# A fused attention and feed-forward kernel: the first pixel chunk loaded uncast through SyncE and cast in SBUF

## The chip, the cores and the metric

The kernel runs on one core of one Trainium2 chip. The core has five engines with a queue of instructions each: TensorE (PE in the profile; PEld is its weight loads), VectorE (DVE), ScalarE (ACT), GpSimd (POOL) and SyncE (SP). SP issues transfers through a hardware queue (q1 in the profile), POOL through a software queue (q0) whose descriptors POOL itself writes; POOL's transfers may change the data type on the way, for instance from float32 to bfloat16. Both queues move their bytes with the same 16 DMA engines. The metric is device time of one execution in microseconds (us), and lower is better.

## The reference

```python
B, C, Hh, Ww = (4, 128, 384, 32)          # q: (B, Hh*Ww, C), kv: (B, Hh, Ww, C), w_sr: (C, C)
kv_pool = kv.reshape(B, H // 4, 4, W // 4, 4, C).mean(axis=(2, 4))
k = v = kv_pool.reshape(B, -1, C) @ w_sr
s = scale * (q @ k.transpose(0, 2, 1))    # scale = 1 / sqrt(C)
a = softmax(s)
x = (a @ v).reshape(B * N, C)             # 49152 tokens
h = x @ w_in                              # w_in: (128, 2048)
out = (h * sigmoid(1.702 * h)) @ w_out    # w_out: (2048, 128)
```

Each image of pixels (`kv`) is averaged in blocks of 4 by 4, which gives 768 keys of 128 channels per image; keys and values are the same matrix. All inputs and the output are float32. The kernel works in bfloat16, with float32 sums.

## The kernel before

**The work.** Queries come in 96 groups of 512 tokens (four groups make a tile of 2048), keys in 6 chunks of 128 per image. For each pair of a group and a key chunk PE makes a 128x512 block of scores (L340), ACT takes the exponential of one to three blocks at once (L342), and PE multiplies the result with the values (L353). DVE divides by the sums and writes the tokens into the large SBUF array `x` (L376 and L379). The second half does the same with the feed-forward layer: PE fills (L586), ACT applies the activation (L588), PE multiplies with the second matrix (L596). The work runs in two rounds (`R = 2`): attention for half of the groups, then their feed-forward, then both once more. Between them the tokens of a round go to DRAM in blocks of 24 x 128 tokens and come back transposed (`put_away`, L493, and `bring_back`, L499, both on SP's queue).

**The order.** The order of every engine's instructions is fixed when the program is built: the list `seq` holds the fills in ACT's order, `first` holds the jobs that are done ahead of each of the first fills, and a small model of times (`now`, `free`, `COST`) places the rest. Waits are put in by the framework where data depend on each other. Each transfer that POOL or SP issues also takes one of eight semaphores in turn, and waits for the transfer that used the same one before.

**The start, which the change touches.** Image 0 comes in six chunks of pixels, `load_chunk(b, jc)` (L126 to L131). A chunk is 128 rows of 2048 values: POOL's transfer reads 1 MB of float32 and writes 512 KB of bfloat16 into a slot of `x`. `XS` is 12, a slot is `SG` = 2048 columns, and chunk `jc` lies in slot 11 - `jc`. Slots 3 to 5 hold the first queries, and slots 0 to 2 hold nothing until attention writes its results there. SP loads the key layer's matrix `w_sr` (L242). POOL issues, in this order (L243 to L256): chunk 0, the queries' first group, their second, chunk 1, two more pieces of queries of two groups each, chunks 2 to 5, more queries, and two casts of queries to DRAM.

While these are under way, DVE builds the identity `ident` from a row of numbers (`row`) and a column (`col`), 32 x 32 at a time (L269 to L273), the mask `sum4` that adds four neighbouring rows (L275 to L277), and the scaled matrix `w_sr_sb` (L279). PE runs 13 warm-up matmuls (`warm(13)`, L291). Then come the jobs of `first`: `pool_chunk(0, 0)` makes 16 matmuls (L139), four (`w`) for each of four blocks of pixel columns (`wp`); DVE copies the sums (L142); `transpose_q(0)` turns the first queries (L233), which ACT copies (L237); `key_chunk` makes the first keys (L148, L149); and so on to the first scores (L340) and exponentials (L342). Chunk 1 is pooled (`pool_chunk(0, 1)`) ahead of the third fill.

**Put away.** `put_away(n, m)` moves block `m` of round `n` in one transfer (768 KB), or in the first round for `m` over `FIRST` = 3 in two of half the size.

Of the kernel before, what the change touches and what calls it, by code (L numbers as in the profile page):

```python
# [7 lines left out]
F32 = mybir.dt.float32  # L8
# [4 lines left out]
AX = mybir.AxisListType  # L13
ADD = mybir.AluOpType.add
MUL = mybir.AluOpType.mult
GE = mybir.AluOpType.is_ge
LE = mybir.AluOpType.is_le
SUB = mybir.AluOpType.subtract
MAX = mybir.AluOpType.max
# [5 lines left out]
def kernel(  # L25
    ctx, tc, q, kv, w_sr, moe_w_in, moe_w_out, out,
):
    nc = tc.nc
    B, N, C = q.shape
    _, H, W, _ = kv.shape  # L30
    r = 4
# [7 lines left out]
    SG = 4 * G  # L39
# [13 lines left out]
    kv_r = kv.rearrange("b (ch p) (a w) c -> b a ch p (w c)", p=128, a=2)  # L53
# [6 lines left out]
    XS = NS // R  # L60
# [24 lines left out]
    def acc(key=None):  # L85

        nonlocal last_acc
        last_acc = next_acc()
        turns.append(last_acc)
        turns.remove(last_acc)  # L90
        if key:
            closes[last_acc] = key
        return banks[:, last_acc, :]
# [15 lines left out]
    x = xpool.tile([128, XS * SG], BF, name="x")  # L109

    def x_tile(s):
        return x[:, s % XS * SG:(s % XS + 1) * SG]
# [5 lines left out]
    kv_tiles, kv_sums, pooled, pTs, kTs, vs = {}, {}, {}, {}, {}, {}  # L118
# [7 lines left out]
    def load_chunk(b, jc):  # L126

        a, ch = divmod(jc, HC)
        t = x_tile(XS - 1 - jc)
        nc.gpsimd.dma_start(out=t, in_=kv_r[b, a, ch])  # L130
        kv_tiles[b, jc] = t.rearrange("p (wp w1 c) -> p w1 wp c", w1=r, c=C)  # L131

    def pool_chunk(b, jc):

        ps = acc()
        t = kv_tiles.pop((b, jc))
        for wp in range(4):
            for w in range(r):
                nc.tensor.matmul(ps[:, 32 * wp:32 * wp + 32], t[:, w, wp, :], sum4,  # L139
                                 start=(w == 0), stop=(w == r - 1))  # L140
        pTs[b, jc] = kvtmp.tile([128, 128], BF, name="pTc", bufs=2)
        nc.vector.tensor_copy(pTs[b, jc], ps[:, 0:128])  # L142
# [78 lines left out]
    def load_q(s, lo, hi):  # L221
        nc.gpsimd.dma_start(
            out=qs[s].rearrange("p (g e) -> p g e", g=4)[:, lo:hi, :],
            in_=q_flat[s * SG + lo * G:s * SG + hi * G, :].rearrange("(g p i) c -> p g (i c)", p=128, i=4))

    def transpose_q(g):
# [11 lines left out]
        else:  # L238
            nc.vector.tensor_copy(dst, src)

    w_sr_f = cpool.tile([128, C], F32)
    nc.sync.dma_start(out=w_sr_f, in_=w_sr)  # L242
    load_chunk(0, 0)  # L243
    load_q(0, 0, 1)
    load_q(0, 1, 2)
    load_chunk(0, 1)
# [14 lines left out]
    col = cpool.tile([128, 32], F32)  # L261
# [3 lines left out]
    row = cpool.tile([128, 32], F32)  # L265
    nc.vector.transpose(row, col)
    ident = cpool.tile([128, 128], BF)
    nc.vector.memset(ident, 0.0)
    for m in range(0, 128, 32):  # L269
        p = slice(m, m + 32)  # L270
        nc.vector.tensor_tensor(ident[p, p], row[p], col[p], EQ)
        if m > 0:
            nc.vector.tensor_scalar_add(row[p], row[p], float(m))  # L273
    sum4 = cpool.tile([128, 32], BF)
    nc.vector.scalar_tensor_tensor(row, col, -float(r), row, MUL, ADD)  # L275
    nc.vector.tensor_scalar(col, row, 0.0, None, GE)
    nc.vector.scalar_tensor_tensor(sum4, row, r - 1.0, col, LE, MUL)  # L277
    w_sr_sb = cpool.tile([128, C], BF)
    nc.vector.tensor_scalar_mul(w_sr_sb, w_sr_f, 1.0 / (r * r))  # L279

# [63 lines left out]
    def drain_attn(t, a):  # L344
# [18 lines left out]
        if k == TS - 1 and a == 1:  # L363
            close(("av", u), max(now, dve - 1.0) + EVACUATE)
            on_dve(6.5 if split else 4.3)
            ps = av_of.pop(u)[:, 0:TS * (C + 1)]
            if split:
                part = parts[:, u, 0:TS * (C + 1)]
                nc.vector.tensor_tensor(part, ps, part, ADD)
                ps = part  # L370
                if u == SPLIT - 1:
                    kept = 0
                    order.clear()
            ps = ps.rearrange("p (k c) -> p k c", k=TS)
            rec = npool.tile([128, TS], F32, name="rec")
            nc.vector.reciprocal(rec, ps[:, :, C])  # L376
            n, o = divmod(u * TS, RT)
            to = x[:, o * T:(o + TS) * T].rearrange("p (k c) -> p k c", k=TS)
            nc.vector.tensor_tensor(to, ps[:, :, 0:C], rec.unsqueeze(2).broadcast_to([128, TS, C]), MUL)  # L379
            if n and (o + TS) % PART == 0:  # L380
                m = o // PART
                put_away(n, m)
                if m:
                    bring_back(n, m - 1)
                if m == RT // PART - 1:
                    bring_back(n, m)
# [100 lines left out]
    PART, FIRST = 24, 3  # L487

    def put_away(n, m):
        size = PART // 2 if n == 0 and m > FIRST else PART  # L490
        for o in range(m * PART, m * PART + PART, size):
            lo = n * XS * SG + o * T
            nc.sync.dma_start(out=x_bf[lo:lo + size * T, :].rearrange("(k p) c -> p k c", p=T),  # L493
                              in_=x[:, o * T:(o + size) * T].rearrange("p (k c) -> p k c", k=size))
# [22 lines left out]
    def background(i):  # L517

        first_round = i < GB * 2
        s = TURN.get(i, NS) if first_round else i // 4 + 3 if i % 4 == 0 else NS  # L520
        if s < NS:
            load_qT(s)
        if i in CAST:
            gate()
            for s in CAST[i]:
                cast_q(s)
        if i in (10, 12):
            gate()
            for jc in range(i % 10 * 3 // 2, i % 10 * 3 // 2 + 3):
                load_chunk(1, jc)  # L530
        if 0 <= i - 16 < JC:
            extras.append((key_and_value, 1, i - 16))
        if 0 <= i - 15 < JC:
            extras.append((pool_chunk, 1, i - 15))
        if i in (28, 33, 38):
            put_away(0, (i - 28) // 5)
        if i in (31, 36, 41):
            bring_back(0, (i - 31) // 5)
        if i == 27:
            gate()  # L540
            nc.gpsimd.dma_start(out=w_in_sb, in_=moe_w_in)
        if i == 28:
            gate()
            nc.gpsimd.dma_start(out=w_out_sb, in_=moe_w_out.rearrange("(o p) c -> p o c", p=128))

    def background_moe(g):

        n, g = divmod(g, 4 * XS)
        m, odd = divmod(g - 9, 2)
        m += FIRST  # L550
        if n == 0 and FIRST <= m < RT // PART:
            (bring_back if odd else put_away)(n, m)
        g += n * 4 * XS
        nonlocal low
        if g == 12:
            low = EARLY * JC
            order[:] = [f for f in order if f >= low // K]
        if g in CAST_MOE:
            gate()
            cast_q(CAST_MOE[g])  # L560
        if g in (41, 42):
            load_qT(g - 28)
        if g == 43:
            background(early[0])
        for b, lo in ((2, 2), (3, 24)):
            if lo <= g < lo + 8:
                gate()
                add_kv(b, g - lo)
            if g in (lo + 10, lo + 12):
                use_kv(b, (g - lo - 10) // 2)  # L570
# [76 lines left out]
    for n in range(R):  # L647
        part = [c for c in chunks if c[0] // (NG // R) == n]
        while part:
            m = sizes.pop(0) if sizes else K  # L650
# [12 lines left out]
        while flat:  # L663
            m = K if len(flat) > sum(rest) else rest.pop(0)
# [36 lines left out]
    def prepare(p):  # L701
# [12 lines left out]

    first = {
        0: [(pool_chunk, 0, 0), (transpose_q, 0), (warm, 1), (key_chunk, 0, 0), (transpose_q, 1)],
        1: [(value_chunk, 0, 0), (warm, 1)],
        2: [(pool_chunk, 0, 1), (warm, 2), (key_and_value, 0, 1), (warm, 1), (transpose_q, 2)],
        3: [(transpose_q, 3)],
        4: [(transpose_q, 4)],  # L720
# [66 lines left out]
    for n in range(len(seq)):  # L787
        fill(n + 2)
        jobs(n + 3)
        while True:  # L790
# [33 lines left out]
            kind, i, c = source[0]  # L824
# [58 lines left out]
```

The softmax here doesn't subtract the row's maximum and nothing guards it: scores larger than these inputs give would overflow.

## Time and profile before

| what | us |
|---|---|
| median of 4 runs (951.1 to 951.33) | 951.22 |
| the profiled execution's own time | 951.1 |
| its span, first to last instruction | 949.3 |
| PE busy / ACT busy | 936.0 / 934.0 |
| DVE busy / POOL busy | 537.0 / 67.1 |
| chunk 0 from POOL's issue at 1.27 to its landing | 5.4 |
| other chunks, issue to landing, median | 10.3 |
| put away, 768 KB / 384 KB, issue to landing, median | 5.9 / 4.6 |

The profile covers one execution of the program. Its page gives each engine's busy time, DMA queues, the chain of work that ended last, and the costliest groups of instructions. Of any stretch one can ask for the list of instructions in order of time (start, length, engine, line, operation, output and inputs, count; in brackets how long the engine had been idle and what released it), for the chain of waits, for each group's mean duration by shape, for busy times by window, and for what the DMA engines moved in 40 equal slices. "L139" is line 139 of the kernel. A matmul's end is modelled, so neighbouring matmuls overlap in the list. DMA sizes and rates count the bytes as written.

### The profile page before, as it was taken

The page shows a single profiled execution, that of the slowest core. Times are in us where ns is not written, and L with a number is a line of the kernel's source. Part 1 is how long each engine was busy: PE and PEld are TensorE (multiplying, and loading weights), DVE is VectorE, ACT ScalarE, POOL GpSimd, SP SyncE. Part 2 cuts the span into 40 slices and gives each one's busy share as a digit, 9 for nine tenths or more (in the row PEclk, how much of TensorE's full clock was granted, in tenths as well). Part 3 has the DMA queues.
Part 4 walks back from the last instruction along what each step waited for, and adds up shares of the span by engine and source line. Part 5 has one row for each costly group of instructions (what it writes and reads, how often), then busy time and mean ns, then how long its engine had stood idle before and what let it go on. Part 6 is the DMA issues. An engine that isn't in the chain of part 4 may idle for free.

```text
span 949.3 us, 15311 instructions
## 1 busy us (share of the span) xinstructions
PE 936.0 (99%) x6201; PEld 503.0 (53%) x6314; DVE 537.0 (57%) x1037; ACT 934.0 (98%) x708; POOL 67.1 (7%) x115
## 2 busy tenths in 40 slices
PE   8999999999999999999999999999999999999998
PEld 4677776444444444444446777754444444444444
DVE  5643553102477777778655775465666665566631
ACT  5999999999999999999999999999999999999998
POOL 4101001330000242000000000000000000000000
PEclk9999999999999999999999999999999999999999
DMA  9999922999766899765335583562222222222222
GB/s 182 207 176 193 212 59 41 157 125 180 153 133 102 126 146 126 123 103 77 66 55 112 131 162 76 135 122 34 44 34 45 34 46 34 45 33 45 34 45 45
DMA packets 372871, 94.93 MB, mean 100 GB/s; under 512 B 346736, under 2 KB 370416, under 8 KB 372464
## 3 DMA queue, kind: packets, MB, share of 16 engines
q1 hardware_dynamic: 343872, 61.31, 36.8%
q0 software_dynamic: 28656, 32.51, 22.5%
q8 instruction: 49, 0.80, 0.4%
q14 instruction: 22, 0.18, 0.1%
q10 hardware_dynamic: 272, 0.13, 0.0%
HBM read 52.49 MB, written 48.76 MB: 107 GB/s over the span
## 4 chain that ended last, share of the span: by engine, by line
ACT 88%; PE 9%; DMA 2%; issue 1%; DVE 0%; POOL 0%; POOLq 0%
ACT ag L588 71%; ACT ag L342 17%; PE banks L340 4%; PE banks L353 3%; DMA qT<-q_bf 1%; DMA x<-in_kv_dram 1%; PE banks L139 0%; PE banks L586 0%; PE banks L624 0%; ACT L588 0%; PE banks L233 0%; PE banks L596 0%; ACT L342 0%; DVE kT L163 0%; PE banks L161 0%
## 5 line engine op out<-in xcount | busy, mean ns | idle before, releaser
L588 ACT ACTIVATE ag<-banks 128x1536 bf16<-128x1536 f32 (+1 forms) x510 | 682.2, 1508 | 0.0
L586 PE MATMUL banks<-x,w_in_sb 128*128 128x512 bf16 x1485 | 407.4, 379 | 2.0 <-ACT ag L588 0.3
L596 PE MATMUL banks<-ag,w_out_sb 128*128 128x512 bf16 x1476 | 403.2, 379 | 1.9
L342 ACT ACTIVATE ag<-banks 128x1536 bf16<-128x1536 f32 (+2 forms) x192 | 245.8, 1442 | 4.2 <-PE banks L233 2.6
L596 PEld LDWEIGHTS <-w_out_sb 128*128 128x128 bf16 x1520 | 148.5, 98 | 178.0 <-issue 0.9
L586 PEld LDWEIGHTS <-w_in_sb 128*128 128x128 bf16 x1522 | 147.3, 98 | 170.4 <-issue 1.1
L607 DVE STREAM_TRANSPOSE o_sb<-banks 128x512 f32<-128x512 f32 x95 | 67.9, 715 | 210.7 <-PE banks L596 195.7
L353 PEld LDWEIGHTS <-ag 128*128 128x128 bf16 x2272 | 146.1, 98 | 46.3 <-issue 0.6
L353 PE MATMUL banks<-v,ag 128*128 128x129 bf16 x2272 | 163.7, 220 | 0.2
L340 PE MATMUL banks<-qT,kT 128*128 128x512 bf16 x499 | 145.0, 379 | 3.5 <-DVE kT L163 1.0
L432 DVE SCALAR_TENSOR_TENSOR ea<-ea,eb 128x512 f32<-128x512 f32 x128 | 87.9, 686 | 3.2
L376 DVE RECIPROCAL rec<-banks 128x3 f32<-128x3 f32 x124 | 22.3, 180 | 95.9 <-PE banks L353 95.9
L379 DVE TENSOR_TENSOR x<-banks,rec 128x384 bf16<-128x384 f32 x124 | 69.2, 558 | 4.3
L340 PEld LDWEIGHTS <-kT 128*128 128x128 bf16 x544 | 46.3, 98 | 26.5 <-DVE kT L163 1.7
L463 DVE RECIPROCAL eb<-ea 128x256 f32<-128x256 f32 x28 | 47.6, 1726 | 0.5
L173 POOL DMA_DIRECT2D kvs<-in_kv_dram x32 | 40.5, 1315 | 19.8 <-DMA kvs<-in_kv_dram 16.3
L421 DVE TENSOR_SCALAR ea<-banks 128x512 f32<-128x512 f32 x32 | 22.1, 692 | 33.1 <-PE banks L405 32.8
L456 DVE SCALAR_TENSOR_TENSOR ea<-ea,eb 128x512 f32<-128x512 f32 x56 | 38.3, 684 | 1.6
L511 POOL MEMSET gate_tile<- 1x1 f32 x37 | 3.9, 105 | 324.6 <-DVE gate_tile L510 324.6
L427 DVE SCALAR_TENSOR_TENSOR eb<-eb,ea 128x512 f32<-128x512 f32 x32 | 22.1, 690 | 0.9
L443 DVE TENSOR_SCALAR qT<-banks 128x512 f32<-128x512 f32 x14 | 9.7, 692 | 17.2 <-PE banks L399 16.9
L434 DVE SCALAR_TENSOR_TENSOR ag<-ea,ee 128x512 bf16<-128x512 f32 x24 | 16.5, 688 | 0.7
(84 smaller groups left out, 267.8 us busy)
## 6 DMA issues: line engine op xcount, KB each, us to landing
out_dram<-o_sb SPq DMA_DIRECT2D x380, 64.0 KB, 2.0
kvs<-in_kv_dram POOLq DMA_DIRECT2D x32, 384.0 KB, 6.4
q_bf<-in_q_dram POOLq DMA_DIRECT2D x21, 512.0 KB, 6.7
x_bf<-x SPq DMA_DIRECT2D x12, 768.0 KB, 5.9
x<-in_kv_dram POOLq DMA_DIRECT2D x12, 512.0 KB, 10.3
x_bf<-x SPq DMA_DIRECT2D x8, 384.0 KB, 4.6
x<-in_q_dram POOLq DMA_DIRECT2D x5, 256.0 KB, 15.5
w_in_sb<-in_moe_w_in_dram POOLq DMA_DIRECT2D x1, 512.0 KB, 10.2
```

The source lines that it names most:

```text
L173: nc.gpsimd.dma_start(out=kv_sums[b][:, i2], in_=kv_p[b, i, w, :, i2], **({"accum_op": ADD} if n else {}))
L340: nc.tensor.matmul(ps[:, k, :], kTs[i // GB][:, jc * 128:(jc + 1) * 128], rhs, start=True, stop=True)
L342: nc.scalar.activation(place([("a",) + c for c in chunks]), ps, AF.Exp, scale=scale)
L353: nc.tensor.matmul(av_of[u][:, k * (C + 1):(k + 1) * (C + 1)], weights(("a", i, jc))[:, o:o + T], vs[i // GB][:, jc, 0:C + 1], start=(jc = ...
L379: nc.vector.tensor_tensor(to, ps[:, :, 0:C], rec.unsqueeze(2).broadcast_to([128, TS, C]), MUL)
L432: nc.vector.scalar_tensor_tensor(a, a, COEFFS[k], b, ADD, MUL)
L456: nc.vector.scalar_tensor_tensor(a, a, COEFFS[k], b, ADD, MUL)
L463: nc.vector.reciprocal(b[:, m:m + 256], a[:, m:m + 256])
L586: nc.tensor.matmul(ps[:, k, :], w_in_sb[:, fc * 128:(fc + 1) * 128], x[:, g % (4 * XS) * G:(g % (4 * XS) + 1) * G], start=True, stop=True)
L588: nc.scalar.activation(place([("m",) + c for c in chunks]), ps, AF.Gelu_apprx_sigmoid)
L596: nc.tensor.matmul(o_of[g], w_out_sb[:, fc, :], weights(("m", g, fc)), start=(fc == 0), stop=(fc == FCH - 1))
L607: nc.vector.transpose(o_sb, o_of.pop(g))
```

## The change

Chunk 0 no longer comes through POOL's queue. SP's queue brings it uncast, 1 MB of float32, ahead of `w_sr`, into slots 0 and 1 of `x`, seen as float32. Once it has landed, five copies turn it into bfloat16 and put it where it was before: DVE casts columns 0 to 511, 512 to 1023 and 1792 to 2047, ACT casts 1024 to 1535 and 1536 to 1791. The blocks of pixel columns (`wp`) of this one chunk are pooled in the order 0, 2, 1, 3. The mask `sum4` is taken from `ident` with one maximum over four neighbouring columns, in place of six operations. In the first round, the put-away of block 4 goes in one transfer and only blocks over 4 go in two.

```diff
-        for wp in range(4):
+        for wp in (0, 2, 1, 3) if (b, jc) == (0, 0) else range(4):
...
+    first_f = x[:, 0:2 * SG].bitcast(F32)
+    nc.sync.dma_start(out=first_f, in_=kv_r[0, 0, 0])
     w_sr_f = cpool.tile([128, C], F32)
     nc.sync.dma_start(out=w_sr_f, in_=w_sr)
-    load_chunk(0, 0)
     load_q(0, 0, 1)
...
         nc.vector.tensor_tensor(ident[p, p], row[p], col[p], EQ)
-        if m > 0:
-            nc.vector.tensor_scalar_add(row[p], row[p], float(m))
     sum4 = cpool.tile([128, 32], BF)
-    nc.vector.scalar_tensor_tensor(row, col, -float(r), row, MUL, ADD)
-    nc.vector.tensor_scalar(col, row, 0.0, None, GE)
-    nc.vector.scalar_tensor_tensor(sum4, row, r - 1.0, col, LE, MUL)
+    nc.vector.tensor_reduce(sum4, ident.rearrange("p (j k) -> p j k", k=r), AX.X, MAX)
+
+    def cast_first():
+
+        t = x_tile(XS - 1)
+        for lo, hi, copy in ((0, 512, nc.vector.tensor_copy), (1024, 1536, nc.scalar.copy), (512, 1024, nc.vector.tensor_copy),
+                             (1536, 1792, nc.scalar.copy), (1792, 2048, nc.vector.tensor_copy)):
+            copy(t[:, lo:hi], first_f[:, lo:hi])
+        kv_tiles[0, 0] = t.rearrange("p (wp w1 c) -> p w1 wp c", w1=r, c=C)
+
+    cast_first()
     w_sr_sb = cpool.tile([128, C], BF)
     nc.vector.tensor_scalar_mul(w_sr_sb, w_sr_f, 1.0 / (r * r))
...
-        size = PART // 2 if n == 0 and m > FIRST else PART
+        size = PART // 2 if n == 0 and m > FIRST + 1 else PART
```

The order of PE's instructions is otherwise what it was, and so is that of ACT, DVE and POOL. On SP's queue one transfer is added at the front and one is gone at block 4.

## The prediction

> **What bounds the kernel now.** I read the page's busy shares first, then the list of ACT's instructions over the first 60 us, then the chain of waits over the first 13 us, and then DMA, PE, POOL and DVE in that stretch.
>
> ```profile
> PE 936.0 (99%) x6201; PEld 503.0 (53%) x6314; DVE 537.0 (57%) x1037; ACT 934.0 (98%) x708; POOL 67.1 (7%) x115
> ```
>
> ```profile
> 0.76 1.28 ACT L237 ACT_TABLE_LOAD   x1 [0.76 <-PEq L867]
> 7.77 0.58 ACT L237 COPY qT<-banks 128x512 bf16<-128x512 bf16 x1 [5.73 <-PE banks L233]
> 9.03 1.29 ACT L342 ACTIVATE ag<-banks 128x512 bf16<-128x512 f32 x2 [0.67 <-PE banks L340]
> 12.92 48.04 ACT L342 ACTIVATE ag<-banks 128x1024 bf16<-128x1024 f32 x44 [2.60 <-PE banks L233]
> ```
>
> The first four fields are start, length, engine and line; the bracket is the idle time before and its releaser. From 12.92 us on ACT runs without a gap that counts: all its waits in the span sum to 11.6 us (5.7, 2.6, 1.3, 1.2 and 0.8), of which 9.8 lie ahead of 12.92. The end is therefore 12.92 plus a sum of ACT work that the change leaves alone. What moves the third exponential (12.92) moves the end, one for one, as long as PE can keep up behind it.
>
> What puts it at 12.92? In the chain of waits (start, length, what) and in PE's list:
>
> ```profile
> 1.27 0.69 POOL x L130
> 1.96 1.03 POOL x L222 x2
> 2.99 7.44 DMA x<-in_kv_dram
> 10.43 0.05 issue
> 10.48 0.57 PE banks L139 x16
> ```
>
> ```profile
> 0.97 5.73 PE L284 MATMUL banks<-ones 128*32 128x512 bf16 x13 [0.97 <-DVE col L262]
> 6.68 0.58 PE L139 MATMUL banks<-sum,x 128*128 128x32 bf16 x16
> 9.30 0.39 PE L340 MATMUL banks<-qT,kT 128*128 128x512 bf16 x1
> 10.48 0.57 PE L139 MATMUL banks<-sum,x 128*128 128x32 bf16 x16 [0.79 <-DMA x<-in_kv_dram]
> ```
>
> It is the landing of the second pixel chunk at 10.43: PE had finished its last score matmul at 9.30 + 0.39 = 9.69 and stood 0.79 us before pooling that chunk. The first chunk is pooled at 6.68, where the 13 warm-up matmuls end. Their weight loads stand 0.43 us apart (the last three before the gap at 4.79, 5.21 and 5.64) and ends are modelled, so pooling could begin two steps after 5.64, at about 6.50, not before.
>
> The DMA view from 1 to 8 us, in 40 slices of 0.175 us:
>
> ```profile
> GB/s 0 0 0 0 67 228 79 0 0 70 164 70 70 23 23 117 164 211 140 281 234 211 187 211 164 211 234 170 146 170 199 205 193 205 211 263 240 222 234 257
> w_sr_f<-in_w_sr_dram SPq DMA_DIRECT2D x1, 64.0 KB, 1.8
> ```
>
> SP's key matrix moves from the fifth slice (1.7 to 1.9 us); POOL's queue starts in the tenth (2.6 to 2.75), crawls until 4.0 (88 GB/s over 2.6 to 4.0), then runs full. From 8 to 16 us the mean is 209 GB/s, and the bytes counted are the written ones (512 KB for a chunk): a cast chunk costs 524,288 / 209,000 = 2.51 us, a 128 KB query piece 0.63.
>
> **What the change moves, with prices.**
>
> *The transfer.* Chunk 0 leaves POOL's queue and becomes the first on SP's (0.76 issue, first bytes 1.8). POOL drops one issue of 0.69; its first query piece takes that place at 1.27, so its bytes still start near 2.65. Uncast it writes 1 MB. No row shows so large an uncast read, so bounds: if the reading side limits, it costs what the same 8 KB rows cost with the cast, 2.51 us; if the writing side, 1,048,576 / 209,000 = 5.02. Between lies the key matrix on the same queue: 3.4% of 7 us for 65,536 bytes is 0.238 us, 275 GB/s, or 3.81 us for 1 MB, but in rows of 512 B. I take 2.51, since rows, packets per engine and source are those of the cast chunk.
>
> From 1.8 to 2.7 it runs alone (0.9 of 2.51); 1.61 remain. If it keeps the engines it ends at 4.3; if it shares them half and half with POOL's queue, at 2.7 + 3.22 = 5.9. Completion adds 0.6 (before: 0.12 MB by 4.0 and the rest at 200 GB/s ends at 6.0, pooled at 6.68). Landing 4.9 to 6.5; I take the middle, 5.7. At 3.81 us with sharing: 2.7 + 5.8 + 0.6 = 9.1; at 5.02: 11.5.
>
> *The second chunk.* The same bytes' worth of work stands ahead of it, but work starts at 1.8 plus the matrix's 0.24 instead of 2.65, which brings 0.6 us; the crawl of POOL's queue (1.4 us at 88 instead of 209, so 0.8 us lost) can now lie under chunk 0, which would make 1.4. It lands at 10.43 less 0.6 to 1.4: 9.0 to 9.8.
>
> *The casts.* DVE's nearest rows are one-source operations in SBUF, 128x512: L429 0.421, L423 0.439 (from PSUM, L421: 0.692, the other end); a quarter of that size, L279, 0.219. So 0.42 + 0.42 + 0.29 for 256 columns = 1.13 us. ACT: 0.60 (its 512-column exponential, 0.597) + 0.37 (between 0.265 for 128 and 0.60) = 0.97, beside it and in an ACT that was idle until 7.77. From 5.7 on: ACT 6.67, DVE 6.83. POOL generates descriptors then, and beside it DVE's one-source rows were longer:
>
> ```profile
> 3.80 0.50 DVE L273 TENSOR_SCALAR row<-row 32x32 f32<-32x32 f32 x1
> 4.33 0.19 DVE L275 SCALAR_TENSOR_TENSOR row<-col,row 128x32 f32<-128x32 f32 x1
> 4.55 0.45 DVE L276 TENSOR_SCALAR col<-row 128x32 f32<-128x32 f32 x1
> ```
>
> L276 is 0.26 over L275 at the same size. I add 0.26 once (7.09); for the far end 0.692 and 0.26 on every cast make about 2.5 us. The Trainium skill ("SBUF — State Buffer", its note on the "DVE blocks DMA" trap) speaks against this edit: such an fp32 copy in SBUF and the GpSimd's descriptor writing exclude each other for whole instructions. By that rule, each cast could also stand behind a whole POOL issue; with the issue row of 0.55, three times, the casts would end at 5.7 + 1.13 + 1.65 = 8.5, not 7.09. The row, with its 0.26, decides for me.
>
> *Pooling.* Its 16 matmuls run as the casts come and end some 0.25 after the last: 7.35, against 7.26. But the query transposes had waited 0.17 for their piece, which now comes earlier. So nothing is gained or lost up to 9.69: shift s = 0 (bounds: -0.4, where warm-up ends; + the lateness of chunk 0).
>
> *The sum.* PE pools chunk 1 at max(9.69 + s, landing 9.0 to 9.8) = 9.7 instead of 10.48: 0.8 us less. Behind it the third exponential needs the queries' next piece, which landed at 11.9 and moves with its queue; chunk 2, for which PE stood 0.46 at 15.5, comes 0.6 to 1.4 earlier and wants 0.8.
>
> *At no cost.* DVE's six removed mask operations (0.37 x3, 0.19, 0.45, 0.19; one reduction, taken as 0.2, comes instead) lie under the warm-up, as before; were that cover gone they would gain 1.7 us. DVE's key-matrix scaling now queues behind the casts and its matrix lands behind chunk 0; the key matmul wants it at 7.98, some 0.7 us after DVE is done. POOL's wait of chunk 4 on chunk 0 (0.83) goes; the queue is full, so it costs or brings nothing. The fifth block put away goes in one transfer of 768 KB (5.9 us to land) instead of two of 384 (4.6 each, the second issued at 228.5). SP issues the transposing read-back at 233.38; 228.0 + 5.9 = 233.9, so SP and the four output transfers behind it may stand 0.5 us. Three output buffers and a block not read until many microseconds later cover that; without cover, 0.5 us.
>
> The sum against the profiled 951.1 us (span 949.3 and 1.8 around it) is 950.3. The median before, 951.22, is 0.12 higher, so the forecast is **950.4**.
>
> **Rivals.** (1) *The first chunk is late* (the other side): SP's uncast transfer is priced like the key matrix, 3.81, and shared half with POOL's. Landing 9.1, casts 1.4, pooling ends 10.75: s = +3.5, chunk 1 pooled at 13.2, 2.7 us later than before: **954.0**. For it: the same-queue row, and queues sharing engines; against: its rows are a sixteenth as long. It costs from a landing of 6.4 on, and 1.9 us from 8.3 on. (2) *VectorE's casts stand behind POOL*: 2.5 us from 5.7, pooling ends 8.45, s = 1.2, chunk 1 at 10.9: **951.6**. For it the 0.50 and 0.45 rows; against, that L279 ran in 0.219 under the same POOL. (3) *Hidden anyway*: sharing puts chunk 0 at 6.5, s = 0.8, or chunk 2 is no earlier and PE stands there instead: **951.2**. (4) *All at its best*: s = -0.4, chunk 1 pooled at 9.3: 1.2 us, **950.0**.
>
> **How the numbers follow.** 0.2% is 1.9 us, about what a measurement of this kernel can tell from no change. Chances: forecast 0.45, (4) 0.15, (3) 0.13, (2) 0.13, (1) 0.10; 0.04 for something else on either side. A gain over 1.9 us would need chunk 1 pooled at 8.58, ahead of the score matmul at 9.30 that PE does first, with s of -1.1; the warm-up forbids it. So faster 0.03, slower 0.12, same 0.85. The range reaches from (4), less 0.1, past (2): 949.9 to 952.0, with (1) left out; the forecast's own is 950.1 to 950.7.
>
> **What would show it.** Right: chunk 0's casts start at 5 to 6.5; the first pooling matmuls start at 6.5 to 6.7 and the second chunk's at about 9.7, without a DMA wait; the third exponential at about 12.1; no new ACT gap behind it. Wrong: first casts after 6.5 (sharing or writing limits), DVE casts over 0.6 us (POOL), PE's wait for chunk 2 over 1 us, or an ACT gap near 230 us (the put-away).

## The result and the profile after

The changed kernel takes 950.35 us (median of 41 runs, 949.74 to 952.11); the kernel before takes 951.22 (61 runs, 950.44 to 952.52). The ratio is 0.999, with a 95% interval of 0.9986 to 0.9995, so the gain of 0.87 us lies between about 0.5 and 1.3. That is inside the 0.2% (1.9 us) that the prediction called "same", and 0.05 us from its 950.4.

| | before | after |
|---|---|---|
| median, us | 951.22 | 950.35 |
| profiled execution / its span | 951.1 / 949.3 | 949.74 / 947.9 |
| ACT starts the casts of chunk 0 | - | 5.71 |
| PE starts pooling chunk 0 | 6.68 | 6.39 |
| PE starts pooling chunk 1 | 10.48 | 9.67 |
| third exponential starts | 12.92 | 12.11 |

ACT in the changed kernel, in order of time (start, length, engine, line; in brackets the idle time before and its releaser):

```profile
0.76 1.28 ACT L281 ACT_TABLE_LOAD   x1 [0.76 <-PEq L874]
5.71 0.93 ACT L281 CAST x<-x 128x512 bf16<-128x512 f32 x2 [3.67 <-DMA x<-in_kv_dram]
7.41 0.58 ACT L237 COPY qT<-banks 128x512 bf16<-128x512 bf16 x1 [0.77 <-PE banks L233]
8.67 1.29 ACT L349 ACTIVATE ag<-banks 128x512 bf16<-128x512 f32 x2 [0.67 <-PE banks L347]
12.11 58.99 ACT L349 ACTIVATE ag<-banks 128x1024 bf16<-128x1024 f32 x52 [2.15 <-PE banks L233]
```

The two casts fill time in which ACT waited before. Chunk 0 has landed by 5.71, and the third exponential, which sets the end, starts at 12.11 instead of 12.92: 0.81 us. The first exponential moved by 0.36 only (8.67 against 9.03).

PE and DVE of the changed kernel over the same stretch:

```profile
6.39 0.74 PE L139 MATMUL banks<-sum,x 128*128 128x32 bf16 x16
8.24 0.39 PE L347 MATMUL banks<-qT,kT 128*128 128x512 bf16 x1 [0.16 <-DVE kT L149]
8.94 0.39 PE L347 MATMUL banks<-qT,kT 128*128 128x512 bf16 x1
9.67 0.56 PE L139 MATMUL banks<-sum,x 128*128 128x32 bf16 x16 [0.34 <-DMA x<-in_kv_dram]
```

```profile
3.12 0.29 DVE L274 TENSOR_REDUCE sum<-ident 128x32 bf16<-128x128 bf16 x1
5.71 1.15 DVE L281 CAST x<-x 128x512 bf16<-128x512 f32 x3 [2.31 <-DMA x<-in_kv_dram]
6.79 0.21 DVE L286 TENSOR_SCALAR w_sr_sb<-w_sr_f 128x128 bf16<-128x128 f32 x1
7.18 0.29 DVE L142 CAST pTc<-banks 128x128 bf16<-128x128 f32 x1 [0.17 <-PE banks L139]
```

PE still waits for the DMA before the second chunk (0.34 in the bracket): the landing, at 9.62, decides when it is pooled, not PE and not the casts.

The profiled spans differ by 1.4 us, more than the 0.81. The rest is a gap of 0.54 us on ACT at 102 us in the profile before, which the profile after does not have. PE stands there before a score block for DVE (L405 before, L412 after), whose queries come by a transposing load that SP issues 7 to 8 us earlier; first before, then after:

```profile
100.84 0.39 PE L405 MATMUL banks<-qT,kT 128*128 128x512 bf16 x1 [0.47 <-DMA qT<-q_bf]
99.48 0.39 PE L412 MATMUL banks<-qT,kT 128*128 128x512 bf16 x1
```

This gap is taken up below.

The DMA view of the changed kernel, first from 1 to 8 us in slices of 0.175 us, then, in the second fence, from 2.6 to 5:

```profile
GB/s 0 0 0 0 281 374 47 47 94 140 187 374 374 328 421 515 328 609 281 515 281 468 266 269 234 237 211 193 193 193 228 281 222 234 211 211 257 164 257 164
x<-in_kv_dram SPq DMA_DIRECT2D x1, 1024.0 KB, 4.9
x<-in_q_dram POOLq DMA_DIRECT2D x2, 128.0 KB, 5.2
```

```profile
DMA packets 117, 0.88 MB, mean 367 GB/s; under 512 B 3, under 2 KB 10, under 8 KB 10
q1 hardware_dynamic: 117, 0.88, 89.6%
```

and from 3 to 5, with the end of the slow stretch left out:

```profile
DMA packets 108, 0.81 MB, mean 403 GB/s; under 512 B 3, under 2 KB 10, under 8 KB 10
```

The uncast chunk begins in the same slice in which the key matrix began before, crawls for some 0.9 us (47 to 187 GB/s), and then writes about twice as many bytes per second (403 GB/s) as cast ones did before (209). Between 2.6 and 5 us all bytes are SP's: POOL had issued its first query piece at 1.27, and nothing of it moved before about 5.1, when chunk 0 was nearly through.

### The profile page after: what moved, and what is told of

Read it like the earlier page. It is cut to its first block, busy times and chain, and to the rows that moved or that the text cites. A ratio compares the mean times of both kernels' runs of the same rounds, so it can differ in the third digit from the quotient of the medians.

```text
span 947.9 us, 15310 instructions
## 1 busy us (share of the span) xinstructions
PE 935.5 (99%) x6201; PEld 503.1 (53%) x6314; DVE 536.4 (57%) x1035; ACT 934.9 (99%) x710; POOL 66.6 (7%) x114
## 4 chain that ended last, share of the span: by engine, by line
ACT 92%; PE 6%; DMA 1%; issue 0%; DVE 0%; POOL 0%; POOLq 0%
ACT ag L595 71%; ACT ag L349 21%; PE banks L347 2%; PE banks L360 2%; DMA x<-in_kv_dram 1%; PE banks L593 0%; PE banks L631 0%; PE banks L139 0%; ACT L595 0%; PE banks L233 0%; PE banks L603 0%; ACT L349 0%; DVE kT L163 0%; POOL x L222 0%; PE banks L161 0%
```

## The experiments

Twelve runs. A median of 11 runs against the runs of the kernel before on the same chip is uncertain by some 0.8 us either way, as much as the whole gain. So the verdicts rest on the profiles: where PE starts to pool chunk 1, where the third exponential starts, and what gap ACT has near 102 us.

| kernel | chunk 1 pooled | third exponential | gap near 102 | span | median | before, same chip | ratio, interval |
|---|---|---|---|---|---|---|---|
| before | 10.48 | 12.92 | 0.54 | 949.3 | 951.22 | - | - |
| before again | 10.87 | 13.31 | 0 | 949.0 | 950.85 | 951.03 | 0.9999 (0.9990 to 1.0008) |
| rest alone | 10.46 | 12.89 | 0 | 949.0 | 951.31 | 951.00 | 1.0005 (0.9996 to 1.0014) |
| uncast by POOL | 10.48 | 12.91 | 1.24 | 950.3 | 951.49 | 951.00 | 1.0004 (0.9995 to 1.0013) |
| after | 9.67 | 12.11 | 0 | 947.9 | 950.35 | 951.22 | 0.9990 (0.9986 to 0.9995) |
| after again | 9.78 | 12.21 | 0.22 | 948.2 | 950.21 | 951.07 | 0.9993 (0.9984 to 1.0002) |
| transfer alone | 9.85 | 12.29 | 1.48 | 950.1 | 950.77 | 951.00 | 0.9999 (0.9990 to 1.0007) |
| matrix first | 10.17 | 12.61 | 0.35 | 948.9 | 950.68 | 951.00 | 0.9999 (0.9990 to 1.0008) |
| casts on DVE | 9.73 | 12.15 | 0.17 | 948.2 | 950.53 | 951.03 | 0.9996 (0.9988 to 1.0005) |
| two halves | 10.11 | 12.55 | 0.26 | 949.5 | 951.05 | 951.03 | 0.9999 (0.9990 to 1.0008) |
| more bytes | 11.08 | 13.52 | 0 | 950.0 | 951.91 | 951.03 | 1.0008 (1.0000 to 1.0017) |
| second chunk sooner | 9.26 | 12.95 | 0.43 | 949.4 | 950.50 | 951.07 | 0.9995 (0.9986 to 1.0003) |
| group 44's block later | 10.34 | 12.77 | 0.42 | 949.3 | 950.53 | 951.07 | 0.9995 (0.9986 to 1.0003) |
| group 38's block later | 9.89 | 12.33 | 0 | 948.0 | 949.92 | 951.05 | 0.9987 (0.9978 to 0.9996) |

Two things can be read from the columns. The third exponential follows the pooling of chunk 1 by 2.42 to 2.44 us in all kernels but "second chunk sooner". And the span less the third exponential's start less the gap is 935.7 to 935.8 us in the two profiles of the kernel before and the two of the changed one: what comes behind is the same work. Over all rows it is 935.7 to 936.7. That spread is as large as the gain; part of it is a wait of 0.2 us on ACT at 23 to 24 us, which four kernels show, and part the time from ACT's last instruction to the end, 3.2 to 3.7 us.

A third regularity joins the first two marks. With the changed kernel's order of transfers, chunk 1 was pooled 3.93 to 3.98 us after the casts of chunk 0 had started, whether these started at 5.71 or at 6.40. With the key matrix ahead of chunk 0 it was 3.72. In the kernels where POOL brings chunk 0 (by the start of its pooling, or of its casts) it was 3.76 to 3.80. That is what the prediction's prices give for the transfers between the two landings: two query pieces and a chunk, 0.63 + 0.63 + 2.51 = 3.77, and 0.24 more where the matrix lies between. So these runs differ in when chunk 0 lands, and what follows is steady.

**Transfer alone.** Mask and put-away as before; the transfer, the casts and the pooling order of the change.

```diff
+        if m > 0:
+            nc.vector.tensor_scalar_add(row[p], row[p], float(m))
-    nc.vector.tensor_reduce(sum4, ident.rearrange("p (j k) -> p j k", k=r), AX.X, MAX)
+    nc.vector.scalar_tensor_tensor(row, col, -float(r), row, MUL, ADD)
+    nc.vector.tensor_scalar(col, row, 0.0, None, GE)
+    nc.vector.scalar_tensor_tensor(sum4, row, r - 1.0, col, LE, MUL)
-        size = PART // 2 if n == 0 and m > FIRST + 1 else PART
+        size = PART // 2 if n == 0 and m > FIRST else PART
```

> Only the transfer through SP, its casts and the pooling order of the change; mask and put-away as before. Theory (the gain is the second chunk's earlier landing, because the DMA engines start on the hardware queue 0.9 us earlier): second chunk pooled near 9.67, third exponential near 12.1, time about 0.8 us under the kernel before, as the whole change. Rival (mask or put-away carry part of it): the third exponential at 12.3 or later, or a time within 0.3 us of before.

Chunk 1 was pooled at 9.85 and the third exponential came at 12.29, between the theory's 12.1 and the 12.3 from which the rival was to count; the median was 0.23 under before, which is the rival's "within 0.3". By these numbers alone it is no clear verdict. The stage lies within the spread of the unedited change (9.67 and 9.78 in its own two profiles, 9.89 and 10.34 in two kernels whose start is the same), and this profile has the largest gap at 102 us, 1.48. The next run decides it from the other side.

**The rest alone.** The kernel before with the new mask and the new put-away.

```diff
+    nc.vector.tensor_reduce(sum4, ident.rearrange("p (j k) -> p j k", k=r), AX.X, MAX)
...
+        size = PART // 2 if n == 0 and m > FIRST + 1 else PART
```

> The rest of the change without the transfer: mask by one maximum, fifth block put away in one transfer; the first chunk comes cast through POOL's queue as before. Theory: third exponential at 12.92, time that of before within 0.3 us. Rival (the put-away or the mask carries part of the gain): at least 0.4 us under before.

10.46 and 12.89: as before to 0.03 us, and the median was 0.31 over before, within the uncertainty. The gain of the stage is the transfer's.

**The same bytes by POOL.**

```diff
-    nc.sync.dma_start(out=first_f, in_=kv_r[0, 0, 0])
+    nc.gpsimd.dma_start(out=first_f, in_=kv_r[0, 0, 0])
```

> The changed kernel with the same uncast transfer issued by POOL as its first, all else kept. Theory (what helps is the early start of the hardware queue): bytes start near 2.7, the first chunk lands near 6.7, the casts end near 7.8, the second chunk lands near 10.4 and is pooled there, third exponential near 12.9, time as before within 0.3 us. Rival (an uncast read is itself faster, or casting on the engines is): second chunk pooled at 9.9 or earlier, time 0.5 us or more under before.

Its PE list:

```profile
7.20 0.76 PE L139 MATMUL banks<-sum,x 128*128 128x32 bf16 x16 [0.50 <-DVE x L281]
9.75 0.39 PE L347 MATMUL banks<-qT,kT 128*128 128x512 bf16 x1
10.48 0.56 PE L139 MATMUL banks<-sum,x 128*128 128x32 bf16 x16 [0.33 <-DMA x<-in_kv_dram]
```

As the theory had it: the casts made the first pooling later (7.20 against 6.68), chunk 1 landed where it did before, and the third exponential came at 12.91. The median, 0.49 over before, is within the uncertainty, and the profile has a gap of 1.24. Neither reading uncast nor casting in SBUF gains anything; issuing from the queue that starts earlier does. The changed kernel also spares POOL one issue, which this run puts back. That was not tried alone, but what POOL issued first in the changed kernel moved nothing before 5.1 us, so a still earlier issue would not have moved it sooner.

**The matrix first.**

```diff
+    nc.sync.dma_start(out=w_sr_f, in_=w_sr)
     nc.sync.dma_start(out=first_f, in_=kv_r[0, 0, 0])
-    nc.sync.dma_start(out=w_sr_f, in_=w_sr)
```

> The changed kernel with the key matrix ahead of the first chunk on SP's queue. In the changed kernel the queue crawls at its start (94 to 187 GB/s between 2.2 and 2.9 us). If the crawl belongs to a queue's first packets, the small matrix takes it: the first chunk lands near 5.2, the second near 9.0, PE is ready at 9.33 and decides, third exponential near 11.8, 1.1 us under before. If it belongs to the first large reads, it stays: first chunk lands 0.2 later (5.9), second at 9.6 as in the change, third exponential 12.1 to 12.3, 0.6 to 0.8 us under before.

The DMA view, 1 to 8 us:

```profile
GB/s 0 0 0 0 47 211 117 421 234 94 47 187 94 281 94 515 187 468 328 468 281 468 562 234 562 334 217 123 199 181 205 211 199 299 205 263 211 211 187 211
```

The small matrix ran at once, and the chunk behind it still crawled: the crawl belongs to the first large read, not to a queue's first packets. Chunk 0 was cast from 6.45 and chunk 1 pooled at 10.17, later than either theory had it. All of the 0.5 by which that is behind the changed kernel's profile lies ahead of chunk 0's landing, since chunk 1 followed in 3.72 instead of 3.95. An unedited start had chunk 0 cast at 6.40 ("group 44's block later"), so one profile can't say how much of the lateness is the order.

**All casts on DVE.**

```diff
-(1024, 1536, nc.scalar.copy)
+(1024, 1536, nc.vector.tensor_copy)
...
-(1536, 1792, nc.scalar.copy)
+(1536, 1792, nc.vector.tensor_copy)
```

> The changed kernel with all five casts on DVE. The casts then end near 5.71 + 0.62 + 0.41 + 0.41 + 0.28 + 0.28 = 7.7 instead of 6.87. Theory (second chunk's landing at 9.62 decides, PE ready at 9.33 has 0.3 of slack): PE ready near 10.1, second chunk pooled there instead of at 9.67, third exponential near 12.55, time 0.35 to 0.4 us under before. Rival (casts lie under DMA altogether): third exponential at 12.1, unchanged. Rival (casts cost one for one): third exponential at 12.95.

```profile
6.40 1.30 PE L139 MATMUL banks<-sum,x 128*128 128x32 bf16 x16 [0.95 <-DVE x L281]
9.50 0.39 PE L347 MATMUL banks<-qT,kT 128*128 128x512 bf16 x1
9.73 0.56 PE L139 MATMUL banks<-sum,x 128*128 128x32 bf16 x16
```

My expectation failed and the first rival was right: pooling took 0.56 us longer, the scores came 0.56 later (9.50 against 8.94), and the third exponential stayed at 12.15. PE can issue the next matmul 0.23 us after a score matmul's start, not after its modelled 0.39 (in the changed kernel too: the score matmul of 8.24 is followed by one at 8.47). So in the changed kernel PE was free at 8.94 + 0.23 = 9.17, 0.45 ahead of the landing, and giving ACT two casts costs and brings nothing.

**Two halves.**

```diff
-    nc.sync.dma_start(out=first_f, in_=kv_r[0, 0, 0])
+    for lo in (0, 1024):
+        nc.sync.dma_start(out=first_f[:, lo:lo + 1024], in_=kv_r[0, 0, 0][:, lo:lo + 1024])
```

> The changed kernel with the first chunk in two transfers on SP's queue, each of half the columns (4 KB rows). If the engines serve a queue's packets one by one with POOL's, the first query piece slips in between and the second half lands later than 5.7. If SP's queue goes first as long as it has packets, the halves land near 4.2 and 5.7, the casts of the first begin 1.5 us earlier, PE starts pooling no earlier than 6.4 because of its warm-up, the second chunk still lands near 9.6, third exponential near 12.1, the time is that of the change.

```profile
5.45 0.26 PE L139 MATMUL banks<-sum,x 128*128 128x32 bf16 x4
6.84 0.57 PE L139 MATMUL banks<-sum,x 128*128 128x32 bf16 x12 [1.13 <-ACT x L282]
10.11 0.56 PE L139 MATMUL banks<-sum,x 128*128 128x32 bf16 x16 [0.51 <-DMA x<-in_kv_dram]
```

PE pooled from 5.45, so the warm-up did not forbid it in this run; the second half was cast from 6.17 only and chunk 1 came at 10.11, again 3.94 behind. Of the expectation's two cases it was the first: POOL's packets began at 4.9 us and moved 0.02 MB from 5.0 to 5.2, beside 0.03 MB of SP's, and the second half came later than 5.7. Starting earlier with half the pixels bought nothing. Whether the halves cost anything is open: 10.11 lies within the spread of the unedited start.

**More bytes ahead.**

```diff
     nc.sync.dma_start(out=w_sr_f, in_=w_sr)
+    nc.sync.dma_start(out=x[:, 2 * SG:3 * SG].bitcast(F32), in_=kv_r[0, 0, 1][:, 0:1024])
```

> The changed kernel with one more uncast transfer of 512 KB behind the key matrix on SP's queue, into a slot that nothing reads. Theory (the second chunk's landing, and so DMA work ahead of it, decides): 64 KB more per two packets of each engine, 1.2 to 1.3 us; query pieces and second chunk land that much later, second chunk pooled near 10.9, third exponential near 13.35, time 0.3 to 0.5 us over before. Rival (DMA has slack; PE or the casts decide): third exponential unchanged at 12.1.

Chunk 1 was pooled at 11.08 and the third exponential came at 13.52: pooling 1.41 us later than in the change, and 1.30 later than in its repeat, whose casts started at the same 5.83; I had 1.2 to 1.3. So the DMA engines' work ahead of chunk 1 sets the start of the third exponential, with no slack. The median is 0.88 over before, where I had 0.3 to 0.5; the interval, 0 to 1.6 us, holds both.

**The kernel before once more.**

> The kernel before once more, for a second profile. Its first profile held a gap of 0.54 us on ACT at 102 us behind a transposing load of queries, which the changed kernel's profile does not have. If the gap is chance: third exponential at 12.92 again and no gap near 102, span near 948.7. If it belongs to the kernel: span 949.3 with the gap.

No gap near 102, but a third exponential at 13.31 where I had 12.92: chunk 0 was pooled at 7.11 instead of 6.68, after a wait of 1.78 us for its DMA, and the span was 949.0. Both the landing and the gap vary from run to run.

**Group 44's block later.** Some score blocks are given to DVE, which computes their exponential; PE fills them early.

```diff
-            return (i // GB, jc) in vs and i // 4 - 1 <= group // 4 and
+            return (i // GB, jc) in vs and i // 4 * 4 - (3 if i == 44 else 4) <= group // 4 * 4 + (group % 4 if i == 44 else 0) and
```

> The changed kernel, with the score block that DVE takes from group 44 filled one group later, so that PE does not stand before queries that are still being transposed. In the profiles so far ACT had a gap near 102 us of 0, 0.17, 0.26, 0.35, 0.54, 1.24 or 1.48 us behind that transfer, in both kernels. Theory (the gap is chance in that transfer's landing, and not part of the change): no gap near 102 here, third exponential near 12.15 as in the change, and a median 0.2 to 0.5 us under the changed kernel's. Rival (the gap comes from what the change does): a gap remains, or moves to the later place.

A miss: the block that PE stands before near 100 us is that of group 38, whose queries are loaded at 92.9; the edit moved another. The gap stayed (0.42). Its start is the changed kernel's, and it shows how far that varies: chunk 0 was cast at 6.40 instead of 5.71 and chunk 1 pooled at 10.34. The first large read crawled longer (1 to 8 us, as above):

```profile
GB/s 0 0 0 0 187 281 234 0 47 0 0 47 234 374 374 374 421 468 374 468 281 468 328 468 246 281 296 202 208 214 182 181 176 211 275 193 287 187 281 117
```

**The second chunk sooner.**

```diff
     load_q(0, 0, 1)
-    load_q(0, 1, 2)
     load_chunk(0, 1)
+    load_q(0, 1, 2)
...
-        0: [(pool_chunk, 0, 0), (transpose_q, 0), (warm, 1), (key_chunk, 0, 0), (transpose_q, 1)],
-        1: [(value_chunk, 0, 0), (warm, 1)],
-        2: [(pool_chunk, 0, 1), (warm, 2), (key_and_value, 0, 1), (warm, 1), (transpose_q, 2)],
+        0: [(pool_chunk, 0, 0), (transpose_q, 0), (warm, 1), (key_chunk, 0, 0)],
+        1: [(value_chunk, 0, 0), (warm, 1), (pool_chunk, 0, 1), (transpose_q, 1), (warm, 1), (key_and_value, 0, 1)],
+        2: [(transpose_q, 2)],
```

> The changed kernel with the second chunk ahead of the second query piece in POOL's queue, and pooled ahead of that piece's scores. Theory (the second chunk's landing decides): it lands 0.6 us earlier, near 9.0, is pooled near 9.1, third exponential near 11.7 instead of 12.11, about 0.4 us under the change. Rival (the chain behind the landing is as long with the second queries in it, or the second exponential comes late): third exponential at 12.1 or later, no gain.

It was pooled at 9.26, but the second exponential came at 11.67 and the third at 12.95: the rival held. The busy times by window (us; then PE, PEld, DVE, ACT and POOL busy with counts; then the granted clock, the DMA share and GB/s) of 9 to 12 and 12 to 15 us, this kernel and then the change's repeat:

```profile
9.00:12.00 3.00, 2.44 (x30) 1.63 (x30) 1.40 (x5) 0.60 (x2) 2.02 (x3) 0.86 1.26 211
12.00:15.00 3.00, 2.78 (x16) 1.62 (x15) 1.73 (x3) 2.06 (x3) 0.61 (x2) 0.58 1.07 215
```

```profile
9.00:12.00 3.00, 2.51 (x28) 1.25 (x29) 1.10 (x5) 0.86 (x2) 1.42 (x2) 1.00 1.23 208
12.00:15.00 3.00, 2.71 (x25) 1.50 (x25) 2.51 (x4) 2.79 (x4) 0.52 (x1) 1.00 1.06 213
```

The second queries' transposes, copy and scores now lie behind the landing. The edit also leaves out two of the single warm-up matmuls behind the first pooling, and PE's granted clock was 0.86 and 0.58 here, 1.00 in the repeat. Whether those two matmuls are the reason, and which of the two effects costs more, was not tried apart.

**The change once more.**

> The changed kernel once more, for a second profile and for times on the same chip as the two others. Theory: second chunk pooled at 9.6 to 9.9, third exponential at 12.1 to 12.3, time about 0.8 us under before; a gap near 102 us of any size between 0 and 1.5.

9.78, 12.21 and a gap of 0.22; 0.86 us under before on the same chip.

**Group 38's block later.** The last edit, on the block that it was meant for.

```diff
-            return (i // GB, jc) in vs and i // 4 - 1 <= group // 4 and
+            return (i // GB, jc) in vs and (group >= 33 if i == 38 else i // 4 - 1 <= group // 4) and
```

> The changed kernel with the DVE-made score block of group 38 filled 24 matmuls later on PE, about 2.3 us (the edit before this one moved group 44's block, which is not the one that stands before the load at 92.9 us). The waits seen there were up to 1.48 us. Theory (that gap is chance in the transposing load's landing, in both kernels): PE has no DMA wait and ACT no gap near 102 us; the time behind the third exponential is shorter by the mean gap of some 0.4 us than in the kernels that have it. Rival: the gap moves with the block or a new one opens when DVE is late with the block.

ACT from 50 to 150 us, first in the kernel before, then here:

```profile
48.59 52.96 ACT L342 ACTIVATE ag<-banks 128x1536 bf16<-128x1536 f32 x39
102.09 40.52 ACT L342 ACTIVATE ag<-banks 128x1536 bf16<-128x1536 f32 x30 [0.54 <-PE banks L340]
```

```profile
49.26 92.08 ACT L349 ACTIVATE ag<-banks 128x1536 bf16<-128x1536 f32 x68
```

No gap, no DMA wait on PE there. The thirteen profiles with the block at its old place have gaps of 0 to 1.48 us, 0.39 in the mean; four of them have none, so this profile alone shows little. Its 11 runs lie between 949.68 and 950.25, those of the kernel before on the same chip between 950.45 and 952.97, and the ratio's interval lies below 1. It has the lowest median here: 1.13 us under before, and 0.43 under the changed kernel's 950.35. The changed kernel was not run on that chip, and the intervals of the two ratios overlap, so that this edit adds to the change is likely but not shown.

## Why the prediction was right, by its own steps

**What bounds the kernel: right.** Once the gap at 102 us is taken out, the end followed the third exponential one for one, to 0.15 us in the two profiles each of before and after and to 1.0 us over all. The prediction counted ACT's waits behind 12.92 in one profile (1.8 us) and did not see that one of them, 0.5, is a draw that comes out between 0 and 1.5.

**The landing of chunk 0: right number by luck, two errors that cancelled.** 5.7 was forecast as the middle between full and half sharing; 5.71 was measured. But there was no sharing with POOL's queue at all, and the crawl, which the prediction hoped to hide, hit chunk 0 itself. Past the crawl the uncast chunk went at 403 GB/s, so 1,048,576 bytes cost 2.60 us, near the 2.51 assumed and far from the 3.81 of the key matrix.

**The second chunk: right.** 9.0 to 9.8 was forecast; PE pooled it at 9.67 to 9.89 in four of the five profiles with the change's start, and at 10.34 in the fifth. The fifth lies outside, and so does the 9.89 by a little; no term of mine held the crawl's spread.

**Which of the two decides: wrong, with the same number.** The sum took PE's 9.69 + s with s = 0, the landing being hidden. It measured s = -0.36 (8.94 against 9.30), about the bound given for it: the pooling of chunk 0 ended at 7.13, not 7.35, and the transposes no longer stood 0.17 for their queries. And PE is free 0.16 earlier than its modelled end says, so PE was ready at 9.17 and the landing at 9.62 decided. Had both been known, the sum would have been the landing's range, 9.0 to 9.8. The number came out because its upper part and 9.69 are neighbours, which is luck. The sign "without a DMA wait" failed with it: PE waited 0.34.

**Casts: right in size; why one was longer is open.** 1.13 on DVE and 0.97 on ACT were forecast, 1.15 and 0.93 measured. One cast had an excess: DVE's first took 0.62 us against 0.41 for the second, 0.21 more, where 0.26 was charged. That is just over the 0.6 that was to be a sign against the prediction, and it cost nothing. The charge was put down to POOL, and this is not shown. The three casts took 1.15 us when they started at 5.71, 1.04 at 5.83 and 0.96 at 6.40, and POOL's row of issues ended at 6.1, which fits. But in "uncast by POOL" they took 0.97 from 6.71 on with POOL issuing beside them from 6.97. By the note on the "DVE blocks DMA" trap in "SBUF — State Buffer" of the Trainium skill, as the prediction read it, each cast could have stood behind a whole POOL issue (0.55); here the casts ended at 6.86, not at 8.5. And "casts on DVE" shows that even 0.56 more would have cost nothing.

**Warm-up as a bound: wrong, without effect.** The prediction let the warm-up set the 6.68 of the first pooling. It was the landing of chunk 0, as the weight loads of the kernel before show:

```profile
6.68 0.48 PEld L139 LDWEIGHTS <-x 128*128 128x128 bf16 x16 [0.89 <-DMA x<-in_kv_dram]
```

In that kernel's second profile the warm-up was over at 5.33 and PE stood 1.78 us before that landing. "Not before 6.50" was too late too: the changed kernel pooled at 6.39, when DVE's first cast was done, and "two halves" at 5.45. There the warm-up's weight loads stood 0.43 us apart up to 3.93 and about 0.21 apart from 4.27 on, where in the changed kernel they stood 0.43 apart to the last, at 5.64. The granted clock reads 1.00 in both, so it does not say why.

**Put-away, mask, scaling: right.** The transposing read-back follows the issue of the one transfer by 232.09 - 226.61 = 5.5 us, against 5.4 before; so it came 0.1 us later, not 0.5, and ACT had no gap there. "Rest alone" puts the rest at nothing in the stage.

**The rivals.** A late first chunk needed sharing, and there was none. For casts behind POOL there is at most the 0.2 us of one cast. "Hidden anyway" was wrong in the profile pair, but a long crawl brings it about in single runs: 10.34 against 10.46.

## What to carry to other kernels

Where one engine is busy to the end, find the instruction from which it never waits again, and ask what lands last before it; only that landing is worth money, and work in front of it (casts, pooling, warm-up) is free until it is later than the landing. At a start-up bound by DMA, it pays to have bytes moving earlier, and to put them on the queue that starts first; which engine cast them did not matter here. When a gain is as small as the spread of the runs, compare the same marks in several profiles and take single random gaps out, before a difference of spans is explained.

## What the runs showed of the hardware that was not expected

- While SP's 1 MB transfer, issued in one piece, was under way, nothing else moved: from 2.6 to 5 us all 0.88 MB were SP's, and the query piece that POOL had issued at 1.27 began at about 5.1. Issued as two halves, it let POOL's packets in from 4.9 on, while the second half was still moving.
- The first large read of the run crawls, on either queue, cast or not, and behind a small transfer too, and its length varies: the same order of transfers had chunk 0 cast at 5.71, 5.83, 5.89, 5.96 and 6.40 us. Why is open.
- One transposing load, the same in each kernel, kept PE, and ACT behind it, waiting between 0 and 1.48 us at about 102 us.
- The 13 equal matmuls of PE's warm-up ended earlier in some runs than in others: the step between them fell from 0.43 to about 0.21 us from 4.27 on in one run and not at all in another, with a granted clock of 1.00 in both.
- With two single warm-up matmuls fewer behind the first pooling, and another order of work, PE's granted clock was 0.58 from 12 to 15 us, against 1.00. The reason was not tried apart.
